# Local attention and a mixture of experts in one kernel: the scale moves into the exponential, row maxima are taken for two units at once, and the routing polynomial runs on GpSimd

## The chip, the core and the metric

The kernel runs on one core of a Trainium2 chip. The metric is the device time of one execution in microseconds. Three timed runs of the kernel before the change took 853.48, 844.39 and 855.21 us; their median, 853.48, is the time before. One more execution was profiled: it took 840.08 us, and its span from the first to the last instruction is 838.4 us, at a mean granted TensorE clock of 0.969. Every moment below is counted from the start of that span.

The engines are called PE or TensorE (matrix products), DVE (VectorE), ACT (ScalarE), POOL (GpSimd) and SP (SyncE, which only issues transfers here). Each works through its own queue of instructions in order.

## The reference

Attention over 4 batches, 8 heads, 768 positions and 64 numbers a head, in which a query sees the first 8 positions and the 95 before it, with a linear bias; then a mixture of 8 experts, of which each token takes two.

```python
scores = (1.0 / np.sqrt(D)) * np.matmul(q, k.transpose(0, 1, 3, 2))
scores = scores + bias[None]                 # -slope of the head * distance
scores = np.where(keep, scores, -1000000000.0)
a = np.exp(scores - np.max(scores, axis=-1, keepdims=True))
a = a / (np.sum(a, axis=-1, keepdims=True) + 1e-09)
x = np.matmul(a, v)                          # 3072 tokens of 512 numbers
noisy = x @ w_gate + np.log1p(np.exp(x @ w_noise)) * noise
top2 = np.argpartition(-noisy, 2, axis=1)[:, :2]   # weights: softmax over the two
h = np.maximum(x[mask] @ w1[e], 0.0)
out[mask] += top2_w[mask, k, None] * (h @ w2[e])
```

## The kernel before

**Blocks, units and steps.** The 3072 tokens are 24 blocks of 128. For a block there are four units (two heads each); a step s of the attention loop works on two units, n = 2s and n+1, so that there are 48 steps (NPR), two to a block, and one more turn of the loop to finish. The loop is written out by hand and software-pipelined. TensorE does in step s the transposes of the probabilities of units n and n+1 (`trans`, L593), the scores of units n+4 and n+5 (`product`: keys times queries at L543, then bias by an identity matmul at L549), and the product with the values for units n-2 and n-1 (`attend`, L617). In odd steps the routing logits of a finished block and its transposes follow (`gate_l` L211, `gate_x` L199), in even steps a transpose of the logits (`gate_s` L220).

**The ring.** The scores of a unit lie in one of three PSUM banks (`scb`). `top` (DVE, L557) takes the row maxima of one unit, negated; `probs` (ACT, L564) computes exp(score + that) into SBUF; only then may the bank be written by a later `product`. `total` (GpSimd, L574 and L576) adds the columns of two units in two steps, `total2` (DVE, L581) finishes the sums, `sums` (L636, L637) takes the reciprocals once a block. `evac` (ACT, L599) copies the transposed probabilities out of PSUM. `heads_out` copies a block's result, one half by DVE (L630), one by ACT (L628). `gate_x2` (DVE, L203) scales it into `xr`, which SP stores to `xd` in DRAM (L191).

**The scale.** The queries are multiplied by 1/8 after their load: `scale_q` at L372 on ACT, L374 on GpSimd for every third piece.

**The routing.** `route(r)` is a Python generator; a `yield` ends a piece, and `tick()` runs one piece of each active route, so that its instructions are spread over the queues between those of attention. There are five routes, for the blocks of SEG; one is started four steps after its last block's. A piece takes the softplus of the noise logits (a polynomial in u/(u+2), L247 to L262, result `ny` at L266), the top two of eight (`max`, `max_index`, L272 and L274), one-hot forms (L285, L288), the position of each token in its expert's list (small matmuls on TensorE, L302 to L306), and writes token number and weight by an indirect DMA to a table in DRAM, two a block (`tbl`, L327, issued by GpSimd: "scatter" below). A tick advances routes 0 and 1 only at every second beat.

**Expert 0 is closed early.** When route CLOSE = 2 has written its entries, the first 512 slots of expert 0 are taken as final: they are read back from the table (`tb0`, L336, on GpSimd's queue) and the rows are gathered from `xd` (L159), so that TensorE can turn them (L176) and begin expert 0 (`up`, L860) when attention ends. The weights of expert 0 are split into a high and a low part meanwhile (L143 on ACT, L144 on GpSimd), one eighth a step from step 18.

**Behind the loop.** The last two routes are finished between the eight `up(0, 0, f)` of expert 0, as `steps_of = [10, 60], [0, 23, 0, 0, 100]` says: pieces of route 3 before f = 0 and 1, of route 4 before f = 1 and 4. For f below 4 the low part of the hidden layer is made by GpSimd (`hl`, L868). Then the whole table is read (L946, L947), the rest of expert 0 is gathered and turned, while three of its four `down` (L893) run; the fourth comes behind those transposes. Experts 1 to 7 follow and keep TensorE busy to the end.

Of the kernel before, what the change touches and what calls it, by code (L numbers as in the profile page):

```python
# [30 lines left out]
def tile_local_global_attention_then_moe(  # L31
# [33 lines left out]
    SEG = [(0, 6), (6, 12), (12, 17), (17, 21), (21, NT)]  # L65
# [115 lines left out]
    NZ = 8  # L181
# [54 lines left out]
    def route(r):  # L236
# [14 lines left out]
        nc.vector.tensor_mul(u, u, t)  # L251
        yield
        nc.vector.tensor_mul(t, u, u)
        yield
        nc.vector.tensor_scalar(p, t, SP_C[7], None, op0=OP.mult)
        yield
        for j in range(6, 0, -1):
            nc.vector.scalar_tensor_tensor(p, p, SP_C[j], t, op0=OP.add, op1=OP.mult)
            yield
        nc.vector.scalar_tensor_tensor(p, p, SP_C[0], u, op0=OP.add, op1=OP.mult)  # L260
        yield
        nc.vector.scalar_tensor_tensor(p, n, 0.0, p, op0=OP.max, op1=OP.add)  # L262
        yield
        nc.vector.tensor_mul(p, p, noise_s[:, a:z])
        yield
        nc.vector.tensor_add(ny, p, l[:, :, :E])  # L266
        yield
        m8 = small.tile([P, SW, 8], F32, name=f"m8{r % 2}")[:, :w]
        ix = small.tile([P, SW, 8], U32, name=f"ix{r % 2}")[:, :w]
        for i in range(w + 1):  # L270
            if i < w:
                nc.vector.max(m8[:, i], ny[:, i])  # L272
            if i:
                nc.vector.max_index(ix[:, i - 1], m8[:, i - 1], ny[:, i - 1])  # L274
            if i % 2 or r <= CLOSE:
                yield
# [4 lines left out]
        yield  # L281
        oh = [small.tile([P, SW, E], F32, name=f"oh{j}{r % 2}")[:, :w] for j in range(2)]
        nc.scalar.activation(wt[:, :, 1], wt[:, :, 1], AF.Exp)
# [39 lines left out]
        for i in range(w):  # L323
            for _ in range(2 if r else 4):
                yield
            for j in range(2):
                ins = nc.gpsimd.indirect_dma_start(  # L327
                    out=tbl, out_offset=bass.IndirectOffsetOnAxis(ap=sli[:, i, j:j + 1], axis=0),
                    in_=ent[:, i, j], in_offset=None, bounds_check=E * TS - 1, oob_is_err=False)
                for o in scat:  # L330
                    tc.declare_no_dep(ins.ins, o.ins, reason="each entry has a slot of its own")
                scat.append(ins)
        if r == CLOSE:

            nc.vector.tensor_scalar(carry[:, 0:1], carry[:, 0:1], float(CA), None, op0=OP.max)
            nc.gpsimd.dma_start(tb0, slots[0, :CA].rearrange("(p t) c -> p t c", t=TA))  # L336
            for _ in range(12):
                yield
            for t in range(TA):
                gather(0, t, DUMP + z * P)  # L340
                yield
# [4 lines left out]
    with ExitStack() as actx:  # L346
# [21 lines left out]

        def scale_q(b, j, i0, eng=nc.scalar):
            t = qs[b, j][:, 2 * i0:2 * i0 + 2]  # L370
            if eng is nc.scalar:
                nc.scalar.activation(t, t, AF.Copy, scale=scale)  # L372
            else:
                nc.gpsimd.tensor_scalar(t, t, scale, None, op0=OP.mult)  # L374
# [15 lines left out]
        if windowed:  # L390
# [34 lines left out]
            def biases(to, d, k):  # L425

                for x in range(2):
                    h = 4 * (k // 2) + 2 * (k % 2) + x
                    nc.vector.tensor_scalar(to[x * Q:(x + 1) * Q, :, k // 2, k % 2], d, -slopes[h], None, op0=OP.mult)
# [26 lines left out]
            scale_q(0, 0, 0)  # L456

            abuf = [ac.tile([P, 2, 3, 2, Q], F32, name=f"a{j}") for j in range(3)]
            scb = [ap.tile([P, 512], F32, name=f"sc{j}") for j in range(3)]
# [59 lines left out]
        def product(n):  # L519
# [5 lines left out]
            for x in range(2):  # L525
                SC[n + x] = scb[(n + x) % 3][:, :2 * w].rearrange("p (y w) -> p y w", y=2)
# [27 lines left out]
        def top(n):  # L554
            g, u, b, i = geo(n)
            MX[n] = aw.tile([P, 2], F32, name="mx", bufs=6)
            nc.vector.tensor_reduce(MX[n], SC[n][:, :, :P + NS] if i else SC[n], op=OP.max, axis=AX.X, negate=True)  # L557

        def probs(n):
            g, u, b, i = geo(n)  # L560
            ps, mx = SC.pop(n), MX.pop(n)
            A[n] = abuf[n // 2 % 3]
            for y in range(2):
                nc.scalar.activation(A[n][:, y, :3 if i else 2, n % 2], ps[:, y].rearrange("p (c t) -> p c t", t=Q),  # L564
                                     AF.Exp, bias=mx[:, y:y + 1])

        def total(n):
# [5 lines left out]
            t = aw.tile([P, 2, 2, Q], F32, name="tot", bufs=2)  # L573
# [48 lines left out]
        def heads_out(g, x):  # L622
            if x == 0:
                OT[g] = gp.tile([P, HP, P], F32, name="ot", bufs=2)
            to = OT[g].rearrange("p (j x) t -> p x j t", x=2)[:, x]
            t = otb[:, x, :2 * P].rearrange("p (j t) -> p j t", t=P)
            if x:
                nc.scalar.activation(to, t, AF.Copy)  # L628
            else:
                nc.vector.tensor_copy(to, t)  # L630
# [106 lines left out]
        else:  # L737
# [4 lines left out]
            for g in range(NT):  # L742
# [4 lines left out]
                if i % NBH == 0 and g + NBH < NT:  # L747
                    nxt = divmod(g // NBH + 1, 2)
                    for k in range(NBH):
                        at(max(n - 2 + 2 * k, 1), load_qk, *nxt, k, 0 if k else NBH)  # L750
                        at(n + 2 * k + 1, scale_q, *nxt, k, nc.gpsimd if k % 2 else nc.scalar)
# [3 lines left out]
            for j in range(NZ):  # L755
                at(NPR - 9 + j, zero_out, j)
            for j in range(2):
                at(38 + 4 * j, load_w)
            for j in range(3):
                at(9 + 5 * j, load_w)  # L760
            for j in range(FC):
                at(18 + j, split, 0, 1, j, nc.gpsimd)
# [3 lines left out]
            top(1)  # L766
# [3 lines left out]
            scale_q(0, 0, 1)  # L770
            product(2)
            top(2)
            top(3)
            for k in range(KC):
                biases(bias, dist, k)
            scale_q(0, 0, 2)
            for s in range(NPR + 1):
# [6 lines left out]
                if odd and s > 1:  # L784
                    heads_out((s - 3) // 2, 0)
                    heads_out((s - 3) // 2, 1)
# [7 lines left out]
                if s + 1 < NPR:  # L794
                    probs(n + 3)
                    total(n + 2)
                if s + 2 < NPR:
                    product(n + 4)
                if s:
                    attend(n - 2)  # L800
                tick()
                tick()
                if s < NPR:
                    total2(n)
                    if odd:
                        sums(s // 2)
                tick()
                tick()
                if s + 2 < NPR:
                    top(n + 4)  # L810
                    tick()
                    top(n + 5)
# [5 lines left out]
                if s == NPR - 1:  # L818
                    for x, _ in [y for y in active if y[1] <= CLOSE]:
                        for _ in x:  # L820
                            pass
                if s >= NPR - 1:
                    for t in (2 * (s - NPR + 1), 2 * (s - NPR + 1) + 1):
                        turn(0, t, scb[t % 3])
# [4 lines left out]
                tick()  # L829
                tick()  # L830
                tick()
# [5 lines left out]
            for x in range(2):  # L837
                heads_out(NT - 1, x)
# [251 lines left out]
```

## Time and profile before

| | us |
|---|---|
| median of three timed runs | 853.48 |
| profiled execution | 840.08 |
| its span | 838.4 |
| first transposes of attention, step 0 | 10.08 |
| first transposes of step 46 | 188.10 |
| first matmul of expert 0 | 216.27 |
| TensorE busy in the span | 770.2 (92%) |
| DVE, ACT, GpSimd busy in the span | 343.2, 324.8, 290.6 |

A row of the timeline has the start of an instruction (or of a run of alike ones), its duration, the engine, the line, the operation, what it writes and reads, how many, and in brackets how long the engine had stood idle before it and what ended that. A row of the groups has line, engine, operation, shapes and count, then busy us and mean ns of one, then the idle time before them. Rows of a stretch have busy us and, in brackets, instructions of each engine.

### The profile page before, as it was taken

What the parts mean: (1) busy time and instruction counts of PE and PEld (TensorE: products, weight loads), DVE (VectorE), ACT (ScalarE), POOL (GpSimd) and SP (SyncE); (2) the same over time, 40 slices, a digit from 0 to 9 for tenths busy, and PEclk for the clock granted to TensorE, in tenths of its full rate; (3) what the DMA queues carried; (4) which work ended last, traced back from release to release, by engine and by line L of the source; (5) the groups of instructions that cost most, each with busy time, mean ns of one, the idle gap of its engine ahead of it and who ended that gap; (6) DMA issues with size and microseconds to landing.
All of it is one profiled execution on the core that took longest, in us unless ns stands there. A gap on an engine that the chain in (4) does not pass through costs nothing. (4 is left out here: it accounts for less than half of the span.)

```text
span 838.4 us, 18068 instructions
## 1 busy us (share of the span) xinstructions
PE 770.2 (92%) x7401; PEld 670.5 (80%) x7401; DVE 343.2 (41%) x872; ACT 324.8 (39%) x705; POOL 290.6 (35%) x315
## 2 busy tenths in 40 slices
PE   5888889784897999999999999999999999999994
PEld 3777767673685998898989888898989889898983
DVE  5477878854540254223413323342333234233300
ACT  3686876552241343233323333332333333233311
POOL 4444776684274313214031412313041222212023
PEclk9899999996897999999999999999999999999998
DMA  8467667792435434335244434434353444432014
GB/s 251 158 234 275 224 181 186 202 243 64 152 92 94 103 112 129 78 94 124 78 98 116 111 100 98 93 98 98 94 119 104 95 94 120 95 76 30 1 25 60
DMA packets 61141, 100.54 MB, mean 120 GB/s; under 512 B 11562, under 2 KB 20010, under 8 KB 61050
## 3 DMA queue, kind: packets, MB, share of 16 engines
q1 hardware_dynamic: 45786, 72.62, 27.9%
q0 software_dynamic: 15264, 26.69, 17.7%
q8 instruction: 60, 0.98, 0.5%
q14 instruction: 31, 0.25, 0.1%
HBM read 71.03 MB, written 28.24 MB: 118 GB/s over the span
## 5 line engine op out<-in xcount | busy, mean ns | idle before, releaser
L878 POOL DMA_INDIRECT out_dram<-y,tba x28 | 44.5, 1588 | 257.6 <-ACT y L877 257.6
L893 PE MATMUL av<-w2h,hh 128*128 128x512 f32 x256 | 103.4, 404 | 0.0
L893 PE MATMUL av<-w2h,hl 128*128 128x512 f32 x256 | 102.2, 399 | 0.0
L893 PE MATMUL av<-w2l,hh 128*128 128x512 f32 x256 | 101.9, 398 | 0.0
L144 DVE TENSOR_TENSOR w1l<-raw,w1h 128x512 fp32r<-128x512 f32 x56 | 38.3, 690 | 148.1 <-ACT w1h L143 148.1
L860 PE MATMUL at<-xh,w1h 128*128 128x512 f32 (+1 forms) x256 | 90.4, 353 | 0.7 <-ACT ot L628 0.7
L860 PE MATMUL sc<-xh,w1h 128*128 128x512 f32 (+1 forms) x256 | 89.7, 350 | 0.0
L878 POOL DMA_INDIRECT out_dram<-y,tbb x24 | 38.1, 1587 | 148.4 <-ACT y L877 148.1
L860 PE MATMUL at<-xh,w1l 128*128 128x512 f32 (+1 forms) x256 | 88.8, 347 | 0.0
L860 PE MATMUL at<-xl,w1h 128*128 128x512 f32 (+1 forms) x256 | 88.8, 347 | 0.0
L860 PE MATMUL sc<-xl,w1h 128*128 128x512 f32 (+1 forms) x256 | 88.4, 345 | 0.0
L860 PE MATMUL sc<-xh,w1l 128*128 128x512 f32 (+1 forms) x256 | 88.4, 345 | 0.0
L564 ACT ACTIVATE a<-sc,mx 128x192 f32<-128x192 f32 (+1 forms) x192 | 68.8, 418 | 42.1 <-DVE mx L557 39.9
L543 PE MATMUL sc<-ks,qbuf 64*64 64x128 f32 (+1 forms) x1408 | 54.3, 267 | 27.6 <-ACT a L564 15.3
L903 PE MATMUL av<-hh,w2h 128*128 128x300 f32 x256 | 78.9, 308 | 0.0
L871 DVE SCALAR_TENSOR_TENSOR hl<-sc,hh 128x300 fp32r<-128x300 f32 (+1 forms) x62 | 35.8, 577 | 101.4 <-ACT hh L870 101.4
L903 PE MATMUL av<-hl,w2h 128*128 128x300 f32 x256 | 77.1, 301 | 0.0
L903 PE MATMUL av<-hh,w2l 128*128 128x300 f32 x256 | 77.0, 301 | 0.0
L543 PEld LDWEIGHTS sc<-ks,qbuf 64*64 64x64 f32 x1408 | 42.1, 143 | 40.8 <-ACT a L564 20.8
L870 ACT ACTIVATE hh<-sc 128x300 fp32r<-128x300 f32 (+1 forms) x62 | 31.4, 507 | 97.2 <-PE sc L860 97.2
L877 ACT ACTIVATE y<-av,tba 128x512 f32<-128x512 f32 x28 | 19.3, 688 | 125.5 <-issue 106.3
L871 DVE SCALAR_TENSOR_TENSOR hl<-at,hh 128x300 fp32r<-128x300 f32 (+1 forms) x62 | 35.8, 578 | 73.9 <-ACT hh L870 73.9
(151 smaller groups left out, 1678.4 us busy)
## 6 DMA issues: line engine op xcount, KB each, us to landing
raw<-in_w SPq DMA_DIRECT2D x32, 1024.0 KB
out_dram<-zero SPq DMA_DIRECT2D x14, 512.0 KB
qbuf<-in_q SPq DMA_DIRECT2D x24, 256.0 KB
vs<-in_v SPq DMA_DIRECT2D x24, 256.0 KB
xd<-xr SPq DMA_DIRECT2D x24, 256.0 KB
ks<-in_k SPq DMA_DIRECT2D x8, 560.0 KB
vp<-in_vb SPq DMA_DIRECT2D x40, 80.0 KB
ks<-in_k SPq DMA_DIRECT2D x6, 432.0 KB
```

Source lines behind the costliest of these rows:

```text
L144: eng.tensor_sub(lo, t, hi.bitcast(F32))
L543: nc.tensor.matmul(SC[n + x][s * Q:(s + 1) * Q, y, c:c + wc], qs[b, j][r, 2 * i0 + s, u + y], m, start=y == 0 and full, stop=False, tile_p ...
L564: nc.scalar.activation(A[n][:, y, :3 if i else 2, n % 2], ps[:, y].rearrange("p (c t) -> p c t", t=Q), AF.Exp, bias=mx[:, y:y + 1])
L860: nc.tensor.matmul(ps, w[:, k, fs], x[c][:, k], start=n == 0, stop=n == 3 * KC - 1)
L870: nc.scalar.activation(hh[c][:, f], ps, AF.Relu)
L871: nc.vector.scalar_tensor_tensor(hl[c][:, f], ps, 0.0, hh[c][:, f].bitcast(F32), op0=OP.max, op1=OP.subtract)
L877: nc.scalar.activation(y, ps, AF.Copy, scale=r[:, 1:2].bitcast(F32))
L878: ins = nc.gpsimd.indirect_dma_start(out=out, out_offset=bass.IndirectOffsetOnAxis(ap=r[:, 0:1], axis=0), in_=y, in_offset=None, bounds_ch ...
L893: nc.tensor.matmul(ps, x[0][:, f, cols], w[:, f], start=n == 0, stop=n == 3 * FC - 1)
L903: nc.tensor.matmul(ps, w[:, f, cols], x[1][:, f], start=n == 0, stop=n == 3 * FC - 1)
```

## The change

It touches attention, the routing and the order of what goes beside them:

- `scale_q` goes. The scores stay unscaled, the biases are divided by the scale, `probs` passes the scale to the exponential, and the maxima are multiplied by it.
- `top` reduces two units at once from one tile of three banks, then multiplies the four numbers a row by the scale with a DVE operation of its own. It is issued directly behind `product`; one tick (even steps) or three (odd) stand ahead of both, three at the step's end: 4 or 6 a step where there were 8.
- `total2` of a pair of units comes a step later, ahead of `product`, with three buffers for the sums.
- The polynomial of a route is issued by GpSimd: 20 operations, with pauses behind them. A tick advances every route, route 2 twice.
- The routes end at blocks 6, 11, 16, 20 and 24, not 6, 12, 17, 21, 24: route 2, which closes expert 0, at block 16. Its `tb0` is loaded on SP's queue, eight pieces later, and the scatters are spaced singly, three or five pieces apart.
- `heads_out` is one copy by ACT.
- Weight loads go to steps 7, 14, 20, 30 and 38; six zero writes go to steps 16 to 36 (there were eight in 39 to 46), the other eight behind the loop; a split of expert 0's weights runs every second step.

```diff
-    SEG = [(0, 6), (6, 12), (12, 17), (17, 21), (21, NT)]
+    SEG = [(0, 6), (6, 11), (11, 16), (16, 20), (20, NT)]
...
-    NZ = 8
+    NZ = 6
...
         nc.vector.scalar_tensor_tensor(u, n, -1.0, n, op0=OP.mult, op1=OP.max)
+        yield
+        yield
         nc.scalar.activation(u, u, AF.Exp, scale=-1.0)
...
         nc.vector.reciprocal(t, t)
         yield
-        nc.vector.tensor_mul(u, u, t)
-        yield
-        nc.vector.tensor_mul(t, u, u)
...
-        for j in range(6, 0, -1):
-            nc.vector.scalar_tensor_tensor(p, p, SP_C[j], t, op0=OP.add, op1=OP.mult)
-            yield
...
+        po_ = nc.gpsimd
+        po_.tensor_mul(u, u, t)
+        po_.tensor_mul(t, u, u)
+        yield
+        po_.tensor_scalar(p, t, SP_C[7], SP_C[6], op0=OP.mult, op1=OP.add)
+        for j in range(5, -1, -1):
+            po_.tensor_mul(p, p, t)
+            po_.tensor_scalar(p, p, SP_C[j], None, op0=OP.add)
+            if j % 2 == 0:
+                yield
+        po_.tensor_mul(p, p, u)
+        po_.tensor_scalar(u, n, 0.0, None, op0=OP.max)
+        yield
+        po_.tensor_add(p, p, u)
+        po_.tensor_mul(p, p, noise_s[:, a:z])
+        po_.tensor_add(ny, p, l[:, :, :E])
+        for _ in range(4):
             yield
...
         for i in range(w):
-            for _ in range(2 if r else 4):
-                yield
             for j in range(2):
+                for _ in range(5 if r == CLOSE else 3):
+                    yield
...
-            nc.gpsimd.dma_start(tb0, slots[0, :CA].rearrange("(p t) c -> p t c", t=TA))
+            for _ in range(8):
+                yield
+            nc.sync.dma_start(tb0, slots[0, :CA].rearrange("(p t) c -> p t c", t=TA))
...
-            active[:] = [(x, r) for x, r in active if r < CLOSE and beat[0] % 2 or next(x, 0) is None]
+            active[:] = [(x, r) for x, r in active if next(x, 0) is None and (r != CLOSE or next(x, 0) is None)]
...
-            MX[n] = aw.tile([P, 2], F32, name="mx", bufs=6)
-            nc.vector.tensor_reduce(MX[n], SC[n][:, :, :P + NS] if i else SC[n], op=OP.max, axis=AX.X, negate=True)
+            ps = scb[:, j[0]:j[1] + 1:j[1] - j[0], :2 * w].rearrange("p x (y w) -> p x y w", y=2)
+            t = aw.tile([P, 2, 2], F32, name="mx", bufs=4)
+            nc.vector.tensor_reduce(t, ps[:, :, :, :P + NS] if i else ps, op=OP.max, axis=AX.X, negate=True)
+            nc.vector.tensor_scalar(t, t, scale, None, op0=OP.mult)
...
-                                     AF.Exp, bias=mx[:, y:y + 1])
+                                     AF.Exp, bias=mx[:, y:y + 1], scale=scale)
...
+            OT[g] = gp.tile([P, HP, P], F32, name="ot", bufs=2)
+            nc.scalar.activation(OT[g].rearrange("p (j x) t -> p x j t", x=2),
+                                 otb[:, :, :2 * P].rearrange("p x (j t) -> p x j t", t=P), AF.Copy)
...
-                at(NPR - 9 + j, zero_out, j)
+                at(16 + 4 * j, zero_out, j)
...
+                at([7, 14, 20, 30, 38][j], load_w)
...
-                at(18 + j, split, 0, 1, j, nc.gpsimd)
+                at(18 + 2 * j, split, 0, 1, j, nc.gpsimd)
...
+                if s:
+                    total2(n - 2)
+                    if not odd:
+                        sums(s // 2 - 1)
                 if s + 2 < NPR:
+                    ticks(3 if odd else 1)
                     product(n + 4)
+                    top(n + 4)
                 if s:
                     attend(n - 2)
-                tick()
-                tick()
-                if s < NPR:
-                    total2(n)
-                    if odd:
-                        sums(s // 2)
...
-                if s + 2 < NPR:
-                    top(n + 4)
-                    tick()
-                    top(n + 5)
...
+                ticks(3 if s < NPR - 1 else 0)
```

In the pieces of queues that the prediction shows, `L562` is the change's `top`, `L276` and `L278` its `max` and `max_index`, `L589` its `total2`, `L333` its scatter, `L255` to `L269` its polynomial, `L859` its `hl`.

More of the change, by code (lines that the diff above doesn't have):

```diff
@@ L340, in route @@
                 gather(0, t, DUMP + z * P)
+                yield
                 yield
@@ L455, in tile_local_global_attention_then_moe @@
                 nc.vector.tensor_copy(identb[x * Q:(x + 1) * Q], ident[x * Q:(x + 1) * Q, x * Q:(x + 1) * Q])
-            scale_q(0, 0, 0)
             abuf = [ac.tile([P, 2, 3, 2, Q], F32, name=f"a{j}") for j in range(3)]
-            scb = [ap.tile([P, 512], F32, name=f"sc{j}") for j in range(3)]
+            scb = ap.tile([P, 3, 512], F32, name="scb")
             atb = ap.tile([P, 2, 512], F32, name="atb")
@@ L525, in product @@
             for x in range(2):
-                SC[n + x] = scb[(n + x) % 3][:, :2 * w].rearrange("p (y w) -> p y w", y=2)
+                SC[n + x] = scb[:, (n + x) % 3, :2 * w].rearrange("p (y w) -> p y w", y=2)
             for y in range(2):
@@ L572, in total @@
                 SUM[g] = aw.tile([P, HP, 2], F32, name="sum", bufs=3)
-            t = aw.tile([P, 2, 2, Q], F32, name="tot", bufs=2)
+            t = aw.tile([P, 2, 2, Q], F32, name="tot", bufs=3)
             nc.gpsimd.tensor_add(t, a[:, :, 0], a[:, :, 1])
@@ L620, in attend, with heads_out @@
                                          skip_group_check=True)
[L622 to L630, printed above, removed]
+        def heads_out(g):
+            OT[g] = gp.tile([P, HP, P], F32, name="ot", bufs=2)
+            nc.scalar.activation(OT[g].rearrange("p (j x) t -> p x j t", x=2),
+                                 otb[:, :, :2 * P].rearrange("p x (j t) -> p x j t", t=P), AF.Copy)
         def sums(g):
@@ L755, in tile_local_global_attention_then_moe, with ticks @@
             for j in range(NZ):
-                at(NPR - 9 + j, zero_out, j)
[L757 to L760, printed above, removed]
+                at(16 + 4 * j, zero_out, j)
+            for j in range(5):
+                at([7, 14, 20, 30, 38][j], load_w)
             for j in range(FC):
-                at(18 + j, split, 0, 1, j, nc.gpsimd)
+                at(18 + 2 * j, split, 0, 1, j, nc.gpsimd)
+            def ticks(n):
+                for _ in range(n):
+                    tick()
             product(0)
             top(0)
-            top(1)
             probs(0)
@@ L784, in tile_local_global_attention_then_moe @@
                 if odd and s > 1:
-                    heads_out((s - 3) // 2, 0)
-                    heads_out((s - 3) // 2, 1)
+                    heads_out((s - 3) // 2)
                     if s > 3:
@@ L818, in tile_local_global_attention_then_moe @@
                 if s == NPR - 1:
-                    for x, _ in [y for y in active if y[1] <= CLOSE]:
-                        for _ in x:
+                    for y in [y for y in active if y[1] <= CLOSE]:
+                        for _ in y[0]:
                             pass
+                        active.remove(y)
                 if s >= NPR - 1:
                     for t in (2 * (s - NPR + 1), 2 * (s - NPR + 1) + 1):
-                        turn(0, t, scb[t % 3])
+                        turn(0, t, scb[:, t % 3])
                 for f, a in todo.pop(s, []):
@@ L836, in tile_local_global_attention_then_moe @@
             xd_store(NT - 2)
-            for x in range(2):
-                heads_out(NT - 1, x)
+            heads_out(NT - 1)
             assert len(routes) == 1 and not todo, (list(routes), list(todo))
```

32 lines of the change are left out of this document (7 added, 25 removed).

## The prediction

> **What bounds the kernel now.** I read the busy time by stage first, then single waits. Columns: stretch in us, its length, busy us and instructions of PE, PEld, DVE, ACT, POOL, granted clock, DMA share, GB/s.
>
> ```profile
> 60.00:120.00 60.00, 51.50 (x1389) 43.03 (x1387) 48.23 (x155) 44.68 (x116) 35.81 (x43) 1.00 0.74 246
> ...
> 180.00:240.00 60.00, 43.29 (x469) 35.12 (x468) 27.18 (x120) 18.66 (x43) 31.59 (x35) 0.83 0.33 100
> ...
> 300.00:320.00 20.00, 20.00 (x109) 17.20 (x108) 8.32 (x14) 9.21 (x17) 7.57 (x6) 1.00 0.60 147
> ```
>
> From 280 us on TensorE is busy all the time, and the diff leaves that code alone, so only the first 270 us can move. There no engine is full: the attention loop is a ring of waits between four queues. Its steps can be told by the first transposes of a step (these start steps 4, 5, 6, 16, 24 and 46):
>
> ```profile
> 30.65 0.82 PE L593 MATMUL atb<-ident,a 128*128 128x128 f32 x6
> 33.22 0.82 PE L593 MATMUL atb<-ident,a 128*128 128x128 f32 x6
> 36.47 0.82 PE L593 MATMUL atb<-ident,a 128*128 128x128 f32 x6
> 70.07 0.82 PE L593 MATMUL atb<-ident,a 128*128 128x128 f32 x6
> 101.60 0.60 PE L593 MATMUL atb<-ident,a 128*128 128x128 f32 x4
> 188.10 0.82 PE L593 MATMUL atb<-ident,a 128*128 128x128 f32 x6
> ```
>
> An undisturbed pair of steps takes 36.47-30.65 = 5.82 us; steps 16 to 46 take 118.0, 7.87 a pair, 16 to 24 31.5, 3.94 a step. The ring in one such step, from product to product:
>
> ```profile
> 109.33 0.67 PE L543 MATMUL sc<-ks,qbuf 64*64 64x128 f32 x21 [0.15 <-ACT a L564]
> 110.47 0.92 DVE L557 TENSOR_REDUCE mx<-sc 128x2 f32<-128x336 f32 x2 [0.98 <-ACT a L564]
> 111.07 0.73 ACT L564 ACTIVATE a<-sc,mx 128x192 f32<-128x192 f32 x2 [0.30 <-DVE mx L557]
> L557 DVE TENSOR_REDUCE mx<-sc 128x2 f32<-128x336 f32 x56 | 25.8, 497 | 4.6 <-PE sc L549 3.5 <-ACT a L564 1.2
> ```
>
> Product to maximum 1.14, one maximum 0.50, hand-over 0.10, probabilities 0.73, hand-over 0.05: 2.52 us. The second maximum lies beside the first probabilities.
>
> **The start.** ACT's scaling of the queries waits for a load there, and TensorE with it:
>
> ```profile
> 22.29 0.63 ACT L372 ACTIVATE qbuf<-qbuf 128x512 f32<-128x512 f32 x1 [4.61 <-DMA qbuf<-in_q]
> 23.59 1.12 PE L543 MATMUL sc<-ks,qbuf 64*64 64x128 f32 x21 [3.47 <-ACT a L564]
> ```
>
> With the scale in the exponential this wait goes (4.6), and two more scalings of 0.63 leave ACT's way: **-6**. If the load is late for its product too, -2.
>
> **The ring.** The maxima of two units become one reduction plus a multiply of four numbers by the scale, both before the first exponential. The reduction reads 672 elements: 0.50 + 336 x 1.04 ns (0.35) = 0.85. The multiply is nearest to this row:
>
> ```profile
> L636 DVE TENSOR_SCALAR sum<-sum x16: 170/172/462, 61.1 to 178.6; 128x8 f32<-128x8 f32 x16
> 141.41 0.71 DVE L289 TENSOR_SCALAR wt<-wt 128x6 f32<-128x6 f32 x1 [0.38 <-ACT wt L283]
> 141.36 0.73 POOL L574 TENSOR_TENSOR tot<-a 128x256 f32<-128x256 f32 x1 [1.17 <-ACT a L564]
> ```
>
> So 0.17, or 0.71 where it meets a GpSimd add: the one that began at 141.41 ended 0.03 us after the add did. The ring becomes 1.14 + 0.85 + 0.04 + 0.17 + 0.10 + 0.73 + 0.05 = 3.08 us, against TensorE's 2.57 and 3.25 in the two steps of the undisturbed pair (33.22-30.65 and 36.47-33.22, transposes to transposes). A pair then needs 3.08 + 3.25 = 6.3. The multiply falls on the moment when `total` starts on GpSimd, so I add half of such an add, 0.35 a step: 3.5. Bounds: 3.1 (never meets it), 3.9 (meets whole adds and the routing on DVE). The Trainium skill, "Advanced Engine Details and Errata", Mode Summary, says that the second VectorE port is shared with GpSimd and that each blocks the other; the L289 row agrees, and without that rule the step would be 3.2 and the loop 9 us shorter.
>
> What DVE loses lies beside this: the copy of `heads_out` (ACT takes it whole), and the wait of `total2` for GpSimd:
>
> ```profile
> DVE sum L581 <- POOL tot L576: 9.8, 9, 3.2
> ACT ot L628 <- DVE ot L630: 10.3, 13, 2.4
> ```
>
> That is what lets steps run at 3.5. Steps 4 to 16, where no routing runs, go from 70.07-30.65 = 39.4 to some 12 x 3.6 (the set-up of table and constants lies there as well): **+4** (bounds -2, +6).
>
> **The polynomial on GpSimd.** Rows for its queue:
>
> ```profile
> L327 POOL DMA_INDIRECT tbl<-ent,sli x48 | 48.7, 1016 | 13.3 <-issue 10.5 <-DVE mx L557 2.1 <-DVE p L258 0.3
> L574 POOL TENSOR_TENSOR tot<-a 128x256 f32<-128x256 f32 x48 | 35.2, 734 | 61.8 <-ACT a L564 59.1 <-DVE mx L557 2.4
> L576 POOL TENSOR_TENSOR tot<-tot,a 128x160 f32<-128x160 f32 x40 | 20.9, 522 | 3.1
> L144 POOL TENSOR_TENSOR w1l<-raw,w1h 128x512 fp32r<-128x512 f32 x8 | 10.2, 1272 | 0.3 <-ACT w1h L143 0.3
> L374 POOL TENSOR_SCALAR qbuf<-qbuf 128x512 f32<-128x512 f32 x7 | 10.6, 1510 | 0.0
> L482 POOL IOTA iota_e<- 128x48 f32 x1 | 0.2, 211 | 0.0
> ```
>
> and, for what DVE paid, one of its steps of the same polynomial:
>
> ```profile
> L258 DVE SCALAR_TENSOR_TENSOR p<-p,t 128x40 f32<-128x40 f32 x6 | 1.1, 190 | 0.1
> ```
>
> A two-input operation costs (734-522)/96 = 2.2 ns an element and 0.17 fixed: 0.27 for 48, and with 0.08 of hand-over to the next of the chain 0.35. Below it stands the 128x48 iota (0.21), above it L374's slope of 2.9 ns (0.40). I take 0.35; 20 rows a route are 7 us where DVE needed some 13 x 0.19. The Trainium skill, "GPSIMD Engine Reference", Engine selection, calls one-input operations roughly line-rate; L374's 1510 ns for 512 is above the two-input L144 row, so this trace disagrees, and by the page a route would take 1 us less. A scatter takes 1.28 (0.97 + 0.30 between), so GpSimd's queue for steps 16 to 45 holds 30 x 0.80 + 26 x 0.55 + 32 x 1.28 + 8 x 1.3 + 75 x 0.35 = 116 us, against 104 before: nearly all of the loop. What counts is the one place per route where DVE waits for the result. DVE in steps 28 and 29, route 1 (ny is the polynomial's result), of the change:
>
> ```order
> L224 TENSOR_TENSOR lh<-lg,rd 128x128
> L226 TENSOR_REDUCE LG<-lh 128x16
> L589 TENSOR_REDUCE sum<-tot 128x2x2
> L276 MAX m_2445<-ny_2195 128x8 x2
> L278 MAX_INDEX ix_2446<-m_2445,ny_2195 128x8
> L276 MAX m_2445<-ny_2195 128x8
> L278 MAX_INDEX ix_2446<-m_2445,ny_2195 128x8
> L276 MAX m_2445<-ny_2195 128x8
> L278 MAX_INDEX ix_2446<-m_2445,ny_2195 128x8
> L562 TENSOR_REDUCE mx<-scb 128x4
> ```
>
> The same place before, where DVE made ny itself:
>
> ```order
> L264 TENSOR_TENSOR p_2431<-p_2431,noise_s 128x48
> L266 TENSOR_TENSOR ny_2432<-p_2431,LG 128x48
> L203 TENSOR_TENSOR xr<-otb,rd 128x512
> L272 MAX m_2770<-ny_2432 128x8
> L581 TENSOR_REDUCE sum<-tot 128x2x2
> ```
>
> Behind the MAX stands `top`, and behind that the ring. GpSimd's way to ny, from the total of step 27: two totals 2.7, two scatters 2.6, a split 1.3, 20 operations 7.0 = 13.6, and 1.3 for a third scatter = 14.9. DVE comes to the MAX two steps and 1 us after the start of step 27, the total starts 2 us after it: 6.0. It waits 8.9. Likewise route 0 (11.0 of queue, no scatters yet) 5, route 2 (advanced twice a tick, 11.7 of queue against 4) 8: 22 us. Steps 16 to 46: 30 x 3.5 + 22 = 127 against 118: **+9** (bounds: 30 x 3.1 + 13 = 106 with operations of 0.21, 30 x 3.9 + 25 = 142).
>
> **Closing expert 0.** Now GpSimd waits for the scatters before it reads the table, and everything waits for GpSimd:
>
> ```profile
> 193.40 0.61 POOL L336 DMA_DIRECT2D tb<-tbl  x1 [2.40 <-DMA tbl<-ent,sli]
> 195.39 0.42 DVE L581 TENSOR_REDUCE sum<-tot 128x4 f32<-128x256 f32 x1 [9.77 <-POOL tot L576]
> 197.76 0.92 PE L617 MATMUL otb<-at,vs 64*64 64x128 f32 x16 [8.84 <-DVE xr L203]
> 201.13 1.00 POOL L159 DMA_INDIRECT xg<-xd,tb  x1 [0.30 <-issue]
> 216.27 0.66 PE L860 MATMUL at<-xh,w1h 128*128 128x512 f32 x1 [0.66 <-ACT ot L628]
> ...
> xg<-xd,tb POOLq DMA_INDIRECT x4, 4.8
> ```
>
> On SP the wait holds only stores of rows that nobody needs yet. Route 2's last scatter now leaves in step 44. From the start of step 46: GpSimd, by the same arithmetic, has polynomial rows of route 3 and the last total until +9.7; then three gathers of 1.3 and three polynomial rows stand before the fourth, which starts at +14.6 and lands 4.8 later; transposes and split add 1.2: the first expert matmul at +20.6, against 216.27-188.10 = 28.2. **-7.5** (bounds -12, 0).
>
> **Behind the loop.** GpSimd after its first hl; before:
>
> ```order
> L868 TENSOR_TENSOR hl_4154<-h,hh_4152 128x512
> L144 TENSOR_TENSOR w2l<-raw,w2h 128x512
> L327 DMA tbl<-ent_4157,sli_4221 25600x2 x8
> L868 TENSOR_TENSOR hl_4154<-h,hh_4152 128x512
> ```
>
> and now, from the same place:
>
> ```order
> L859 TENSOR_TENSOR hl_4045<-h,hh_4043 128x512
> L144 TENSOR_TENSOR w2l<-raw,w2h 128x512
> L333 DMA tbl<-ent_4070,sli_4134 25600x2 x8
> L255 TENSOR_TENSOR u_4160<-u_4160,t_4161 128x32
> L256 TENSOR_TENSOR t_4161<-u_4160 128x32
> ```
>
> The last route's polynomial stands behind the eight scatters of route 3, and TensorE's position matmuls for that route (L302) still stand between the fourth and fifth f of expert 0.
>
> ```profile
> 230.21 0.19 PE L302 MATMUL lg<-ohs,upper 128*128 128x8 bf16 x2
> 241.46 0.39 PE L893 MATMUL av<-w2h,hh 128*128 128x512 f32 x1
> 258.13 0.40 PE L893 MATMUL av<-w2h,hl 128*128 128x512 f32 x1
> ...
> 236.10 1.31 POOL L868 TENSOR_TENSOR hl<-h,hh 128x512 fp32r<-128x512 f32 x1
> 249.06 0.97 POOL L327 DMA_INDIRECT tbl<-ent,sli  x1 [0.30 <-issue]
> 263.37 0.93 PE L176 MATMUL m<-ident,xg 100*128 100x100 f32 x4 [4.83 <-DMA xg<-xd,tbb]
> 266.97 0.78 PE L893 MATMUL av<-w2h,hh 128*128 128x512 f32 x1
> ```
>
> From the first expert matmul (M = 216.27): scatters end at M+19.8, 20 operations of 0.32 later ny at M+26.2, MAX to one-hot 1.8 more: M+28, where TensorE stood at M+13.9: a stall of 14. Behind it 241.46-230.4 = 11 us of `up`, plus 2 at a low clock after the idling (the first matmul after the present stall takes 0.78, not 0.39), and three `down` to 258.4, 16.9: M+58. The gathers have landed by then (eight scatters, not six, and the 13.3 from the last scatter to 263.37: M+56), so the old stall of 4.8 there goes. Fourth `down` at M+60 against 266.97-216.27 = 50.7, less 2 of its own low clock: **+7.5** (bounds +4, +10).
>
> **At nothing.** ACT's `heads_out` of 512 elements adds some 0.2 a pair to a queue that waits anyway (ACT ot above); if that cover goes, 24 x 0.2 = 5. Zero writes, weight loads and the splits of expert 0 move to other steps, with the same count but for two zero writes behind the loop; SP has room, and the split parts are first read by expert matmuls. Were a load late, a product would wait as at 23.59, 3.5 each.
>
> **Sum.** -6 + 4 + 9 - 7.5 + 7.5 = +7 on a span of 838.4, or 847 for the profiled execution's 840.1. The three timed runs have a median of 853.5, 13.4 above it, so: 860.
>
> **Rivals.** (1) *The loop at TensorE's pace*: small GpSimd operations cost an iota's 0.21 and the multiply slips in. Steps of 3.1 and waits of 15: 108 for 16 to 46 (-10), -1 for 4 to 16, +5 behind: -19.5, 834. For it: DVE and ACT lose their waits on each other; against: L574's fixed part. (2) *DVE's queue becomes the bound*: the multiply and every two-input operation wait for a GpSimd that hardly rests, steps of 3.9 as between 70 and 102 now: 117 + 19 of waits (DVE comes later) = 136 (+18), +6, +9.5, -7.5, -6: +20, 873.5. It decides once a step passes 3.7. For it: the L289 row; against: DVE loses its copy and the polynomial. (3) *Closing sooner brings nothing*: the table's load stands on SP behind stores that wait for DVE, and the gathers come as late as now: the -7.5 falls away, 868. For it: the gathers' queue place behind route 3's polynomial; against: SP is nearly empty there.
>
> **Chances.** Forecast 0.42 (own range 847 to 869), (1) 0.23, (2) 0.25, (3) 0.10. Faster by over 2% (under 836.4, about what a measurement here tells from no change): 0.6 of (1) and a little of the forecast, 0.16. Slower (over 870.5): 0.6 of (2), 0.4 of (3), 0.05: 0.24. Within: 0.60. Range 834 to 880.
>
> **What would show it.** Right: no ACT wait for qbuf before 30 us; in each route one DVE wait of 5 to 9 us at the first MAX, released by GpSimd; GpSimd operations of 128x48 at 0.25 to 0.30; the 8.84 gone; TensorE idle some 14 us before the last position matmuls, and no 4.83 afterwards. Wrong: loop steps of 3.1 between routes, MAX waits under 2 us, or an idle GpSimd in steps 16 to 46.

## The result, and the profile after

The change made the kernel slower: 933.96 us median of four runs (933.15 to 936.73) against 848.93 (four runs of the kernel before, the fourth at 843.20), a ratio of 1.101 with a 95% interval of 1.091 to 1.111. The prediction had said 860, with a range of 834 to 880. The profiled execution's span went from 838.4 to 932.0 us.

The same moments as in the prediction, in the changed kernel: first transposes (L601) of steps 4, 5, 6, 16 and 46 and the first matmul of expert 0.

```profile
33.62 0.82 PE L601 MATMUL atb<-ident,a 128*128 128x128 f32 x6
37.84 0.82 PE L601 MATMUL atb<-ident,a 128*128 128x128 f32 x6
43.45 0.82 PE L601 MATMUL atb<-ident,a 128*128 128x128 f32 x6
...
95.15 0.82 PE L601 MATMUL atb<-ident,a 128*128 128x128 f32 x6
...
272.42 0.82 PE L601 MATMUL atb<-ident,a 128*128 128x128 f32 x6
...
295.22 0.76 PE L851 MATMUL at<-xh,w1h 128*128 128x512 f32 x1 [1.50 <-DVE xl L179]
```

An undisturbed pair of steps takes 43.45 - 33.62 = 9.83 us, where 5.82 was measured before and 6.3 to 7 forecast. Taking the differences stage by stage (the last two columns are kernels of the third group of experiments below):

| us | before | after | change | forecast | three score tiles | and the old polynomial |
|---|---|---|---|---|---|---|
| to step 4 | 30.65 | 33.62 | +3.0 | -6 | 26.7 | 26.1 |
| steps 4 to 16 | 39.4 | 61.5 | +22.1 | +4 | 42.6 | 40.9 |
| steps 16 to 46 | 118.0 | 177.3 | +59.2 | +9 | 131.7 | 116.5 |
| step 46 to expert 0 | 28.2 | 22.8 | -5.4 | -7.5 | 25.1 | 18.7 |
| expert 0 to the end | 622.1 | 636.8 | +14.7 | +7.5 | 634.6 | 625.5 |
| span | 838.4 | 932.0 | +93.6 | +7 | 860.7 | 827.6 |

So 81 of the 94 us were lost in steps 4 to 46. One turn of the ring there, all in the changed kernel (start, duration, engine, line, and in brackets what ended the idle time ahead of it):

```profile
50.00 0.75 ACT L572 ACTIVATE a<-scb,mx 128x192 f32<-128x192 f32 x2
50.80 0.88 PE L544 MATMUL scb<-ks,qbuf 64*64 64x128 f32 x32 [2.32 <-ACT a L572]
51.96 0.86 DVE L562 TENSOR_REDUCE mx<-scb 128x4 f32<-128x672 f32 x1 [2.30 <-PE scb L550]
52.85 0.17 DVE L563 TENSOR_SCALAR mx<-mx 128x4 f32<-128x4 f32 x1
53.14 0.73 ACT L572 ACTIVATE a<-scb,mx 128x192 f32<-128x192 f32 x2 [2.39 <-DVE mx L563]
53.30 0.82 PE L601 MATMUL atb<-ident,a 128*128 128x128 f32 x6
54.22 0.81 ACT L607 ACTIVATE at<-atb 128x768 f32<-128x768 f32 x1 [0.18 <-PE atb L601]
54.93 0.73 ACT L572 ACTIVATE a<-scb,mx 128x192 f32<-128x192 f32 x2
55.71 0.88 PE L544 MATMUL scb<-ks,qbuf 64*64 64x128 f32 x32 [1.58 <-ACT a L572]
```

Follow ACT: the first probabilities of a step (53.14) are over at 53.87, but `product` does not start. It starts at 55.71, 0.05 behind the end of the *second* probabilities (54.93 + 0.73), and these stand behind `evac` (54.22) in ACT's queue. Product to product is 4.91 us. Every part but one has the price that the prediction gave it: reduction 0.86 (0.85), multiply 0.17, probabilities 0.73; new is the stretch from 53.87 to 55.66. In the list of waits this is nearly every step:

```profile
DVE mx L562 <- PE scb L550: 98.5, 44, 4.3
PE scb L544 <- ACT a L572: 97.5, 47, 4.9
ACT a L572 <- DVE mx L563: 84.7, 32, 5.2
```

Before the change the product came directly behind the first probabilities of its step, which ended at 109.28, and ahead of the second ones (the product of 109.33 is in the prediction):

```profile
108.53 0.75 ACT L564 ACTIVATE a<-sc,mx 128x192 f32<-128x192 f32 x2
...
109.98 0.79 ACT L564 ACTIVATE a<-sc,mx 128x192 f32<-128x192 f32 x2
```

The banks do not ask for the later start: units n+4 and n+5 go to the banks that n+1 and n+2 leave, and the second probabilities read the bank of n+3. What the banks have in common is that they are one tile now. The programs show it at the first matmul of a `product` (the second row of each pair is what follows: before, the first matmul of the other bank; after, the next matmuls of the same one):

```
L543 MATMUL sc_225<-ks,qbuf_109 64x128 [waits DVE_49]
L543 MATMUL sc_226<-ks,qbuf_109 64x128 [waits DVE_49,Activation_49]

L544 MATMUL scb<-ks,qbuf_110 64x128 [waits DVE_49,Activation_49]
L544 MATMUL scb<-ks,qbuf_110 64x128 x3
```

### The profile page after: what moved, and what is told of

It reads as the page before. It is cut to its first block, busy times and chain, and to the rows that moved or that the text cites. A ratio compares the mean times of both kernels' runs of the same rounds, so it can differ in the third digit from the quotient of the medians.

```text
span 932.0 us, 17968 instructions
## 1 busy us (share of the span) xinstructions
PE 781.2 (84%) x7399; PEld 680.9 (73%) x7399; DVE 328.5 (35%) x783; ACT 321.1 (34%) x688; POOL 306.9 (33%) x407
## 4 chain that ended last, share of the span: by engine, by line
PE 50%; issue 22%; POOL 10%; ACT 8%; DVE 4%; DMA 3%; another core or an unknown queue 1%; POOLq 0%; ACTq 0%; DVEq 0%
PE av L884 10%; PE at L851 9%; PE sc L851 9%; PE av L894 7%; PE scb L544 4%; ACT a L572 4%; ACT at L607 3%; POOL out_dram L869 3%; PE otb L625 2%; PE atb L601 2%; DVE mx L562 2%; POOL tbl L333 2%; POOL xg L159 1%; DMA tbl<-ent,sli 1%; POOL p L261 1%
## 5 line engine op out<-in xcount | busy, mean ns | idle before, releaser
L544 PE MATMUL scb<-ks,qbuf 64*64 64x128 f32 (+1 forms) x1408 | 48.5, 283 | 102.9 <-ACT a L572 97.5
L544 PEld LDWEIGHTS scb<-ks,qbuf 64*64 64x64 f32 x1408 | 40.9, 155 | 114.7 <-ACT a L572 109.4
L572 ACT ACTIVATE a<-scb,mx 128x192 f32<-128x192 f32 (+1 forms) x192 | 68.7, 415 | 127.2 <-DVE mx L563 84.7
L582 POOL TENSOR_TENSOR tot<-a 128x256 f32<-128x256 f32 x48 | 35.0, 730 | 129.1 <-ACT a L572 129.1
L562 DVE TENSOR_REDUCE mx<-scb 128x4 f32<-128x672 f32 (+1 forms) x48 | 39.8, 829 | 100.3 <-PE scb L550 98.5
```

The costliest lines, as they stand in the source:

```text
L544: nc.tensor.matmul(SC[n + x][s * Q:(s + 1) * Q, y, c:c + wc], qs[b, j][r, 2 * i0 + s, u + y], m, start=y == 0 and full, stop=False, tile_p ...
L562: nc.vector.tensor_reduce(t, ps[:, :, :, :P + NS] if i else ps, op=OP.max, axis=AX.X, negate=True)
L582: nc.gpsimd.tensor_add(t, a[:, :, 0], a[:, :, 1])
```

## The experiments

Theory 1 is that a wait is set for the tile as a whole: whatever reads one bank holds back who writes another. Theory 2: the ring is serial because the reduction of both units and the multiply stand ahead of the first exponential. Theory 3: GpSimd's polynomial, and the port that it shares with VectorE, hold every step back. The kernels were run in groups, each on one chip with the kernel before beside it (838.1 us in the first group, 849.5 in the second, 835.0 in the third, 837.5 in the fourth).

### First group: is it the tile?

**Three tiles.**

```diff
-            scb = ap.tile([P, 3, 512], F32, name="scb")
+            scb = [ap.tile([P, 512], F32, name=f"sc{j}") for j in range(3)]
...
-            nc.vector.tensor_reduce(t, ps[:, :, :, :P + NS] if i else ps, op=OP.max, axis=AX.X, negate=True)
+            for x in range(2):
+                ps = SC[n + x]
+                nc.vector.tensor_reduce(t[:, x], ps[:, :, :P + NS] if i else ps, op=OP.max, axis=AX.X, negate=True)
```

> The changed kernel with the scores in three tiles of one bank each, as before the change, and so two reductions and one multiply a step; all else as changed. Theory 1 (product waits for the probabilities of a unit whose bank it does not write, because the three banks are one tile): the wait goes, undisturbed pairs of steps fall from 9.85 us to about 6.5, the time from 934 to 850-870. Theory 2 (the ring is serial because both maxima and the multiply stand ahead of the first exponential): this order is kept, so pairs stay above 9 and the time at 925-940. Theory 3 (GpSimd's polynomial and its port hold DVE back in every step): 925-940.

**One tile, single maxima:** the second half of that diff alone.

> The changed kernel with one tile of three banks as changed, but two single reductions (and one multiply) a step. Differs from the first of these runs by the tile alone. Theory 1: still 9.8 to 10.2 a pair, 930-945. Theory 2 with the pair reduction itself at fault: back to 6.5 a pair, 850-870. Theory 3: 925-940.

**Product ahead of the second probabilities**, one tile and pair reduction kept:

```diff
+                if s + 2 < NPR:
+                    product(n + 4)
                 if s + 1 < NPR:
                     probs(n + 3)
                     total(n + 2)
...
-                    product(n + 4)
```

> The changed kernel, one tile and pair reduction kept, with the call of product one place earlier: ahead of the step's second probabilities instead of behind them. Theory 1: product then waits only for the first probabilities (0.73 + 0.05 + 1.16 + 0.86 + 0.03 + 0.17 + 0.12 = 3.1 a step), the second probabilities wait for product instead, which ends about when evac does: pairs 6.3 to 6.8, 845-870. Theories 2 and 3: nothing changes by more than 1%, 925-940.

**The kernel before, with one tile** and nothing else changed:

> The kernel before with nothing changed but that its three score banks are one tile. Theory 1: product now waits for the second probabilities, which stand behind evac: 0.73 + 0.05 + 1.14 + 0.50 + 0.10 + 0.73 + 0.81 and hand-overs of 0.3 = 4.3 a step instead of 2.9 to 3.9, pairs 8 to 9 instead of 5.82, time 885-905. Theories 2 and 3: 849, as before.

Measured: three tiles 862.3 (1.030 of before, 1.024 to 1.035); one tile with single maxima 927.1 (1.106, 1.099 to 1.112); product ahead 883.7 (1.055, 1.050 to 1.060); the kernel before with one tile 899.0 (1.074, 1.068 to 1.080). The first two differ by the tile alone: 64.8 us. The last differs from the kernel before by it alone: 61 us. Single maxima with one tile came out 3 us under what theory 1 had said (930 to 945), the other two inside it. No loss by the pair reduction is shown: with it and without it the one-tile kernel takes 1.101 and 1.106 of before, inside each other's intervals (933.96 and 927.1 us, measured beside different runs of the kernel before). Theories 2 and 3 fall as causes of these 61 to 65 us, theory 1 holds. The kernel before with one tile, steps 4 to 6, and its wait beside that of the kernel before:

```profile
34.56 0.82 PE L593 MATMUL atb<-ident,a 128*128 128x128 f32 x6
...
44.04 0.82 PE L593 MATMUL atb<-ident,a 128*128 128x128 f32 x6
```
```profile
PE sc L543 <- ACT a L564: 12.8, 10, 3.5
...
PE scb L543 <- ACT a L564: 73.7, 40, 3.0
```

That is 9.5 us a pair where it had been 5.82, and the wait grew from 12.8 us to 73.7.

The Trainium skill, "PSUM — Partial Sum Buffer", section on bank collisions, reports that accesses of two engines to different banks run clean, so by that page too the wait protects nothing; and "Perfetto Trace Analysis", Matmuls, advises rotating matmul groups through banks so that one is read while the next is written. This kernel does rotate, and still had no such overlap: the trace adds that the banks must be tiles of their own.

Product ahead took 43 us off the one-tile kernel with single maxima, and against the changed kernel 50 us by the times or 38 by the ratios. 64 to 89 were expected (845 to 870): a miss, and its trace names the reason (ACT, DVE, PE and POOL of one step):

```profile
31.40 0.88 PE L544 MATMUL scb<-ks,qbuf 64*64 64x128 f32 x32 [0.81 <-ACT a L572]
32.49 0.73 ACT L572 ACTIVATE a<-scb,mx 128x192 f32<-128x192 f32 x2 [0.27 <-PE scb L550]
33.25 0.86 DVE L562 TENSOR_REDUCE mx<-scb 128x4 f32<-128x672 f32 x1 [1.37 <-ACT a L572]
34.10 0.52 POOL L584 TENSOR_TENSOR tot<-tot,a 128x160 f32<-128x160 f32 x1
34.15 0.50 DVE L563 TENSOR_SCALAR mx<-mx 128x4 f32<-128x4 f32 x1
35.53 0.88 PE L544 MATMUL scb<-ks,qbuf 64*64 64x128 f32 x32 [1.49 <-ACT a L572]
```

`product` starts behind the first probabilities now, but the maxima, which only read, wait until the second probabilities have read *their* bank (33.22): the order by tile holds between two readers as well. Not every tile is handled so: in the last kernel of the third group the two maxima of a step are halves of one `mx` tile in SBUF, and its program lets the first probabilities wait for the first maximum alone. What decides between the two, no run here shows. A step is 35.53 - 31.40 = 4.13. And the multiply of four numbers, 0.17 elsewhere, takes 0.50 here: it ends 0.03 us behind GpSimd's addition, as the prediction had it from the L289 row.

### Second and fourth group: what is left of the loss

With three tiles 24 us of loss remain. Theory 4 puts them to the waits for the polynomial on GpSimd. Rival 4a says that VectorE is late anyway and other waits would take their place, rival 4b that GpSimd holds VectorE's port, wherever the MAX stands. All runs of the second group took longer than the same kernels in other groups, by 0.7 to 2.1% (with the table on GpSimd TensorE shows gaps of 0.4 to 0.5 us between the matmuls of `attend`; why is open), so three of its four kernels were run once more beside their standard, and the text goes by these.

**The polynomial on VectorE, in the same lumps:** `po_ = nc.gpsimd` becomes `po_ = nc.vector`.

> The changed kernel with three score tiles and single maxima (the first run, 862.3), and the 20 operations of each routing polynomial on VectorE instead of GpSimd, in the same places. Theory 4 (the waits of VectorE's first MAX for GpSimd's result, some 27 us in steps 16 to 46, and TensorE's 14 us before the last position matmuls are what is left of the loss): both go, against 20 x 0.2 = 4 us of VectorE a route that partly lies in the ring (+6 in all): 825-836. Rival 4a (VectorE is late anyway, other waits take their place): 850-862.

**The first MAX later:** twelve more pauses ahead of it in routes 0 to 2.

```diff
-        for _ in range(4):
+        for _ in range(4 if r > CLOSE else 16):
             yield
         m8 = small.tile([P, SW, 8], F32, name=f"m8{r % 2}")[:, :w]
```

> The first run's kernel with the polynomial left on GpSimd and twelve more pauses between its last operation and the first MAX of routes 0 to 2, so that VectorE comes there about two steps later. Theory 4: the waits in the loop shrink from 27 to under 8 us, closing expert 0 comes 0 to 5 us later, the 14 us behind the loop stay: 840-850. Rival 4b (the cost is GpSimd holding VectorE's second port, wherever the MAX stands): 858-864.

**The queries scaled, as before the change** (`scale_q` back, no multiply, no scale in the exponential):

> The first run's kernel with the scale back where it was: queries scaled after their load (ACT, every second one GpSimd), no multiply behind the maxima, no scale in the exponential. If the multiply costs its 0.17 and half a GpSimd add in every step's ring (0.5 a step), steps 4 to 46 become 20 us shorter and the start 3 longer: 842-850. If it costs its 0.17 alone: -7, +3 and the scalings: 855-862. If the scale's move is worth what was forecast at the start and nothing in the ring: 864-868.

**The table read back on GpSimd's queue:** `nc.sync.dma_start(tb0, ...)` becomes `nc.gpsimd.dma_start(tb0, ...)`.

> The first run's kernel with expert 0's table read back on GpSimd's queue again, all else as in the first run. If SP's queue is what let expert 0 close sooner: the first expert matmul comes 3 to 7 us later behind step 46, 864-870. If closing sooner has nothing to do with the queue of that load: 862, within 3.

These gave 854.1, 859.4, 866.5 and 871.1 beside 849.5. The third, 1.021 of before (1.016 to 1.027), lies 0.8 to 1.0% under the three-tile kernel's ratios, 7 to 8 us: between what a multiply of 0.5 us a step and one of 0.17 had been expected to cost, and near what the same edit gives below. Taken as they stand, the first two times lie in the ranges of rivals 4a and 4b and the third in that of a scale that costs the ring nothing, beside a kernel before that was itself 11 us slower than in the first group. The first, second and fourth once more, beside the three-tile kernel:

> The first run's kernel (three score tiles, single maxima) as the standard for the next three. If absolute times carry over from call to call: 862. If ratios do: 1.030 of the kernel before, whatever that takes here.

> The polynomial on VectorE in five lumps, beside its standard. By the absolute times of before: 8 below the standard. By the ratios: 21 below.

> The polynomial on GpSimd with the first MAX of routes 0 to 2 about two steps later, beside its standard. By the absolute times: 3 below the standard. By the ratios: 15 below. Theory 4 (the waits are 25 us of the loop): 12 to 20 below.

> The table's load back on GpSimd's queue, beside its standard. By the absolute times and the forecast's closing term (-7.5): 7 to 10 above the standard. By the ratios and the prediction's third rival: within 3 of it.

Measured: three tiles 862.1 (1.029, 1.024 to 1.034), lumps on VectorE 836.6 (0.998, 0.996 to 1.000), MAX later 853.6 (1.019, 1.014 to 1.024), table on GpSimd 864.4 (1.031, 1.027 to 1.036). So:

- The polynomial on GpSimd costs 25 us, all that was left: that part of theory 4 holds, and rival 4a falls. By stages it is 8 us in steps 16 to 46, 7 at the closing and 9 behind the loop. With the 13 operations of before, one a piece (below), it is 29. In the slower second group the gain was smaller: lumps on VectorE and table on GpSimd lie 17 us apart there, 28 here.
- Putting the MAX later took 19.5 us of the 23.8 us of waiting away, and steps 16 to 46 became 11.2 us shorter (131.2 to 119.9); closing expert 0 came 3.9 later. It is 8.5 us in all, under the 12 to 20 expected. Part of the wait had only moved: 5.9 us of waiting for GpSimd's totals took its place (steps 16 to 46, three tiles and then MAX later):

```profile
DVE m L276 <- POOL ny L269: 23.8, 3, 10.6
...
DVE sum L588 <- POOL tot L583: 5.9, 3, 2.8
DVE m L276 <- POOL ny L269: 4.3, 1, 4.3
```

- Rival 4b explains little. The operation that met GpSimd above, the multiply of four numbers, took 11.2 us for its 30 executions in the loop with the polynomial on GpSimd and 10.0 with it on VectorE, and `total2` and `gate_x2` took the same (408 and 407 ns, 689 and 688):

```profile
L562 DVE TENSOR_SCALAR mx<-mx 128x4 f32<-128x4 f32 x30 | 11.2, 373 | 1.0
...
L562 DVE TENSOR_SCALAR mx<-mx 128x4 f32<-128x4 f32 x30 | 10.0, 333 | 1.0
```

- The queue of the table's load is worth 2.3 us, not clear of noise (the two intervals overlap): the prediction's third rival, as far as the queue goes. The forecast's way, with a gain of 7 to 10, is not borne out.

### Third group: the parts alone, and a better kernel

**Three tiles again**, as the standard of this group:

> The first run's kernel (three score tiles, single maxima) once more, to stand beside the next three: 862 within 3, or 1.030 of the kernel before within 0.006, whichever of the two carries over.

**The polynomial wholly as before:** on VectorE, 13 operations, one a piece (the three-tile kernel with L244 to L266 of the kernel before).

> The first run's kernel with the routing polynomial as it was before the change: on VectorE, 13 operations, one a piece. The fifth run put 20 operations on VectorE in five lumps. Theory 5 (the lumps stood in the ring, spread they lie beside it): steps 16 to 46 from 131-134 down to 115-122, first expert matmul to the end 622-627 instead of 634, time 15 to 25 below the first run's kernel. Rival 5a (VectorE's queue itself is what the ring waits for): 5 to 10 below it, as in the fifth run.

**The scale alone**, in the kernel before:

```diff
             nc.vector.tensor_reduce(MX[n], SC[n][:, :, :P + NS] if i else SC[n], op=OP.max, axis=AX.X, negate=True)
+            nc.vector.tensor_scalar(MX[n], MX[n], scale, None, op0=OP.mult)
...
-                                     AF.Exp, bias=mx[:, y:y + 1])
+                                     AF.Exp, bias=mx[:, y:y + 1], scale=scale)
```

> The kernel before with one part of the change alone: the scale in the exponential, each single maximum followed by its own multiply of two numbers. By the forecast's terms: -6 at the start, two multiplies of 0.17 on VectorE a step of which one is in the ring, with half a GpSimd add: 0.17 to 0.5 x 43 = 7 to 21, so 1 to 15 slower than before. Rival (the load is late for its product too, the start brings 1): 6 to 20 slower. Rival (the multiply lies beside other waits): 3 to 6 faster.

**Polynomial and scale as before**, with three tiles:

> The first run's kernel with both the polynomial and the scale as before the change; what is left of the change are the sums a step later, the single copy of heads_out, one place for both maxima and the routing's order. If the multiply is what made steps 4 to 16 take 41.7 us instead of 36.9: 3 to 8 below the kernel with the polynomial alone taken back, and not slower than the kernel before. If the scalings on ACT and GpSimd cost as much later: equal to it within 3.

Measured beside 835.0: 861.9 (1.031, 1.026 to 1.037); 832.4 (0.996, 0.993 to 0.999); 839.6 (1.006, 1.003 to 1.010); 825.6 (0.987, 0.981 to 0.993). The second is 29 us below its standard, more than the 15 to 25 expected. The last is 1.3% faster than the kernel before and the fastest of this study. What it keeps of the change: the sums a step later, one copy of `heads_out`, both maxima in one place, the routes' new bounds and pauses, the table on SP. The starts of steps 4, 6 and 16 (polynomial as before, then polynomial and scale as before) show what the multiply costs:

```profile
26.13 0.82 PE L596 MATMUL atb<-ident,a 128*128 128x128 f32 x6
32.79 0.82 PE L596 MATMUL atb<-ident,a 128*128 128x128 f32 x6
66.98 0.82 PE L596 MATMUL atb<-ident,a 128*128 128x128 f32 x6
...
28.75 0.82 PE L604 MATMUL atb<-ident,a 128*128 128x128 f32 x6
34.57 0.82 PE L604 MATMUL atb<-ident,a 128*128 128x128 f32 x6
65.39 0.82 PE L604 MATMUL atb<-ident,a 128*128 128x128 f32 x6
```

Steps 4 to 16 take 40.9 us with the multiply, 36.6 without: 0.36 a step, against 0.17 + 0.35 in the prediction's ring. An undisturbed pair takes 6.66 against 5.82. In the kernel before, where each maximum has its own multiply, the scale alone raises the pair from 5.82 to 6.68, so the wait for both maxima is not needed to explain it. The scale in the exponential gives 2.6 us back at the start (26.1 against 28.8), and in all the kernel is 6.8 us slower for it by the medians (2.8 by the two profiled executions); alone in the kernel before, it is 4.6 slower, within the 1 to 15 expected.

## Why the prediction was wrong

**The failed step is the ring's hand-over of 0.05** from the probabilities to `product`, in "The ring". It was read from a row of the kernel before, `109.33 ... [0.15 <-ACT a L564]`, where three tiles let the first probabilities release the product. The diff made one tile of them; the prediction gave that no price, and none of its rivals had it. The ring is not 3.08 but 4.9 us; the 65 us between the kernels that differ in the tile alone are the larger part of the 94. It also turned the start's gain into a loss: the three-tile kernel is at step 4 after 26.7 us, the changed one after 33.6.

Judged against the three-tile kernel, which does what the prediction thought the change did, the sum was +7 and the profile shows 860.7 - 838.4 = +22. That this kernel's 862 is near the forecast of 860 is luck: 860 stood on a median of 853.5, and beside the three-tile kernel the one before took 835 to 838. By terms:

- **Steps of 3.5: right.** An undisturbed pair is 6.7 (6.3 to 7 forecast). Steps 4 to 16 cost +3.2 (+4 forecast). Take the three waits for GpSimd out of steps 16 to 46 and (131.7 - 25.3)/30 = 3.5 is left; with the MAX later it is (119.9 - 4.3 - 5.9)/30 = 3.7. The multiply's share was dearer in the sum than it came: 0.52 a step against a mean of 0.37 (the row with 11.2 us above).
- **One wait a route at the first MAX: right in place, a little small in size.** Forecast 5, 9 and 8 us, 22 in all; the three-tile kernel waited 25.3, and steps 16 to 46 cost +13.7, not +9:

```profile
86.37 0.24 DVE L276 MAX8 m<-ny 128x8 f32<-128x8 f32 x2 [6.29 <-POOL ny L269]
132.08 0.24 DVE L276 MAX8 m<-ny 128x8 f32<-128x8 f32 x2 [10.61 <-POOL ny L269]
170.68 0.24 DVE L276 MAX8 m<-ny 128x8 f32<-128x8 f32 x2 [8.44 <-POOL ny L269]
```

  The single two-input operations came as priced (0.29 for 48 numbers, forecast 0.25 to 0.30); the six one-input ones of L261 were dearer, 0.33:

```profile
L261 POOL TENSOR_SCALAR p<-p 128x48 f32<-128x48 f32 x6 | 2.0, 332 | 0.5
L260 POOL TENSOR_TENSOR p<-p,t 128x48 f32<-128x48 f32 x6 | 1.7, 286 | 0.5
```

- **The start, -6: mis-sized**, -3.9. The wait for qbuf left ACT, and `product` took it over (5.3 us in the changed kernel), which the prediction had named as what would leave only -2.
- **Closing sooner, -7.5: mis-sized**, -3.1 (-5.4 in the changed kernel). The fourth gather began 15.9 us behind step 46 (14.6 forecast), the first expert matmul 9.2 behind that (6.0). The polynomial of route 3 stands ahead of the gathers on GpSimd; with it on VectorE the fourth one begins at 9.4, and the stretch is 18.7, 9.5 below before. Whether the block sooner or the pauses bring that was not tried apart.
- **Behind the loop, +7.5: mis-sized**, +12 to +15. The stall was forecast at 14 and came at 14.33, its matmul 28.9 behind the first of expert 0 (28 forecast). What failed is the claim that the later stall goes:

```profile
324.12 0.20 PE L308 MATMUL lg<-ohs,upper 128*128 128x8 bf16 x2 [14.33 <-DVE ohs L294]
...
338.07 0.39 PE L884 MATMUL av<-w2h,hh 128*128 128x512 f32 x1
...
357.62 0.93 PE L176 MATMUL m<-ident,xg 100*128 100x100 f32 x4 [2.59 <-DMA xg<-xd,tbb]
...
361.30 0.78 PE L884 MATMUL av<-w2h,hh 128*128 128x512 f32 x1
```

  The gathers landed at 357.62 - 295.22 = 62.4, not 56. Route 4's last scatter ended at 341.03, 45.8 behind the first matmul of expert 0, where the prediction's 56 less its 13.3 stands for 42.7; and from there it took 16.6, not 13.3. 2.6 of the old 4.8 us stayed, and the fourth `down` began at 66.1, not 60.

Of the signs set out to prove it wrong, "an idle GpSimd" was the one that showed: 95.05 us busy in 177.2 in steps 16 to 46 of the changed kernel, where the sum had it at work for 116 of 127.

```profile
95.20:272.40 177.20, 106.83 (x2556) 91.14 (x2554) 80.03 (x277) 76.31 (x194) 95.05 (x160) 0.87 0.40 121
```

## What to carry to other kernels

Buffers that rotate must be objects of their own where waits are set by object, as they were for this score tile: one tile of three banks made each product wait for both probabilities of its step, for 61 to 65 us of 840. When a diff changes how a buffer is declared, list the waits of the first instruction that writes it and of the next reader, before and after; here one name more at one matmul told it. A long chain of small operations moved to a slower engine costs its latency at the one place that needs the result, and again wherever that engine's other work is awaited (here 15 us in the loop, 6 at the closing, 9 behind it).

## What the runs showed of the hardware

A stall can be paid twice: TensorE comes back at a lower granted clock. In the three-tile kernel it stood idle for 9.85 us up to 135.27, and the stretches around that (the clock stands behind the engines, ahead of the DMA share and GB/s) read:

```profile
116.00:124.00 8.00, 7.64 (x196) 6.11 (x190) 4.64 (x13) 5.48 (x14) 6.45 (x13) 1.00 0.95 234
124.00:132.00 8.00, 1.42 (x12) 1.01 (x10) 0.00 (x0) 0.00 (x0) 6.87 (x16) 0.86 0.54 177
132.00:140.00 8.00, 4.73 (x81) 4.41 (x82) 7.11 (x34) 4.06 (x11) 6.82 (x9) 0.50 0.26 7
140.00:148.00 8.00, 7.41 (x225) 6.39 (x227) 6.51 (x26) 5.60 (x14) 3.39 (x6) 1.00 0.59 207
```

The clock is 0.50 of full speed from 132 to 140, and 1.00 again behind. The Trainium skill, "TensorE: Matmul & The Clock Gate", HAM oscillation, puts the point at which an idle TensorE loses its clock at about 3.4 us; the gap of 9.85 agrees. A shorter gap can be followed by the same, as the changed kernel shows, which ran at 0.87 in steps 16 to 46 (the row with 95.05 above):

```profile
56.00:60.00 4.00, 2.35 (x83) 2.03 (x75) 1.91 (x5) 1.96 (x5) 0.98 (x2) 1.00 0.44 134
60.00:64.00 4.00, 3.37 (x84) 3.01 (x84) 1.03 (x2) 0.81 (x3) 1.25 (x2) 0.57 1.03 327
64.00:68.00 4.00, 2.42 (x62) 2.15 (x62) 1.57 (x5) 2.10 (x6) 0.97 (x2) 1.00 0.19 68
```

The longest gap of TensorE in these 12 us is 2.29 us, ended by the product at 60.63. Gaps of 2.29 and 2.32 us, ended at 40.95 and 50.80, had left the clock at 1.00 from 36 to 60. What tells them apart is open.
